# Routed attention and a squared-ReLU MLP on one core: v products in even units of batch 0's second half, plain products in odd ones

## The chip, the cores and the metric

The kernel runs on one core of a Trainium2 chip. The metric is the time of one execution on the device in microseconds (us), the median of five runs. Before the change it is 978.76 us (976.63 to 979.76).

## The reference, cut to what matters

```python
q, k, v: (4, 8, 768, 64)   centroids: (8, 16, 64)   w_in: (512, 2048)   w_out: (2048, 512)
q_assign = argmax(q_n . c_n)          # each query and key belongs to one of 16 clusters
k_assign = argmax(k_n . c_n)
scores = where(q_assign == k_assign, q @ k.T / sqrt(64), -1e9)
attn = exp(scores - max);  attn = attn / (sum(attn) + 1e-9)
x = (attn @ v), heads side by side    # (3072, 512)
out = relu(x @ w_in) ** 2 @ w_out     # (3072, 512)
```

## The kernel before

**Units.** A pair is two heads of one batch: 16 pairs, pairs 0 to 3 are batch 0 (`HP` = 4). The 768 queries of a pair are cut in two halves `h`, the keys in three steps `c` of 256. A unit is (pair, h, c). The list `units` (L718) has the first halves of pairs 0 to 3 (units 0 to 11), then their second halves (12 to 23; `TWOS` = 12), then pairs 4 to 15 with both halves (24 to 95). The main loop at L786 goes through the units. For each it writes, in this order, the score products and exponentials, the v products that are ready, the sums that are complete, the rounding of weights, and some "plain" products.

**Scores** (`scores`, L446). TensorE makes eight products into two PSUM tiles `sc`. ScalarE takes the exponential (L473). In batch 0 the mask is inside the products (one-hot `ohT`), and the exponential writes the tile `ex`, of which there are three buffers. From pair 4 on, the mask is four VectorE operations (L477) which write `ex` and read `qid`, a tile that the preparation of the pair sends through DRAM (`spread`, L400). GpSimd adds up `ex` into `acc` (L487, L489).

**v products** (`times_v`, L504). Four products for each unit, into `av`, accumulated over the three units of a half. The PSUM pool has two such tiles.

**Sums** (`add_up`, L530, and `finish`, L560). When a half is complete, TensorE multiplies the sums by ones into a PSUM bank `sm`, VectorE takes the reciprocal `r` (L544), the SP queue sends it to DRAM (`far_r`, L547, and `seen`, L551) and back spread over the partitions (`rb`, L550), and VectorE multiplies (L563) and so writes `xT`. This L563 also frees the `av` tile.

**Plain products** (`ffn`, L572). The two halves of batch 0 go through the MLP by ordinary matrix products: 64 of 384 columns into a bank `ph` for each half (L577, each followed by two ScalarE operations for every four), then 48 of 512 columns into `po` (L590). They need only `xT` and weights, and `fill_steps` deals them out in columns. `density` says how many parts of them a unit gets: 4 in batch 0, 2 later. The other batches run after the loop (`ffn_pair`, L603).

**Banks.** `sm`, `ph`, `po`, `lg`, `lt` and `pb` share one pool of two PSUM banks (`ps_f`, L79). A product into a new bank waits until the bank before last has been read.

**Rounding of weights** (`round_weights`, L141). 32 blocks, 4 in every 3 units from the start up to unit 23. Each takes two ScalarE operations (L150, L152), three VectorE operations (L155, L159, L162), one GpSimd addition (L166), and then frees one of four buffers `w_raw`, into which the SP queue loads the next block (L139).

**Preparation of a pair** (`prep`, L415). For pair 4 it is a list of fifteen items, three taken in each unit: the transposed load of q and k (`turn_words`, L290), the splitting of the next pair's words (L273), the cluster products `lg` (`logits`, L300), the choice of the cluster (`route`, L313: transposes into `lt`, then VectorE's L344 to L363), and `spread` (transpose `pb`, ScalarE L407, `far` L409, `qid` L410).

**What sets the order.** Each engine, and the SP queue, works in a fixed order which a scheduler makes from the program's order, dependencies and priorities (`together` gives products a high one). An instruction that waits holds up all that stands behind it on its engine or queue. Two places of the loop set which units do what:

```python
elif u == TWOS or u % 2 or u >= len(units):      # L804: v products up to unit u - 1
    ready = u
if u % 2 == 0 or not TWOS < u < len(units):      # L841: plain products for two units
```

So after unit 12 an odd unit has the v products of two units and no plain products, and an even unit has plain products for two units and no v products.

Of the kernel before, what the change touches and what calls it, by code (L numbers as in the profile page):

```python
# [25 lines left out]
def kernel(  # L26
# [14 lines left out]
    NCH = S // P  # L41
# [4 lines left out]
    HP = H // 2  # L46
# [68 lines left out]
    def load_v(pair):  # L115
        b, hp = divmod(pair, HP)
        raw_v[pair] = loads_v.tile([P, 2, NCH, D], F32, name="v_raw")
        nc.sync.dma_start(
            raw_v[pair], v[b, 2 * hp : 2 * hp + 2].rearrange("h (p j) d -> p h j d", p=P)
        )  # L120
# [16 lines left out]
    def load_weights(i):  # L137
        raw_w[i] = wstage.tile([P, NW, 2], U32, name="w_raw")
        nc.sync.dma_start(raw_w[i], weights[i][1])  # L139
# [133 lines left out]
    def split_words(pair, which):  # L273
        if which == 0:
            words[pair] = dram.tile([2 * NCH, P, 2, 2 * D], U16, name="words")
        flat = loads.tile([P, NCH, 2, 2 * D], U16, name="flat", tag="qk")
        src = raw[pair][which].bitcast(U16).rearrange("p c (d two) -> p c two d", two=2)
        half = NCH // 2
        with tc.issue_after(last_exp[0]):
            for cols in (slice(0, half), slice(half, NCH)):  # L280
                nc.scalar.copy(out=flat[:, cols], in_=src[:, cols])
        nc.sync.dma_start(
            words[pair][NCH * which : NCH * (which + 1)].rearrange("c p two d -> p c two d"),
            flat,
        )
        if which == 1:
            raw.pop(pair)
            load_qk(pair + 1)
# [126 lines left out]
    def prep(pair):  # L415
        if pair < HP:
            return [
                lambda: turn(pair, 0), lambda: turn(pair, 1), lambda: turn(pair, 2),
                lambda: logits(pair), lambda: route(pair),
                lambda: turn_onehot(pair, 0), lambda: turn_onehot(pair, 1),  # L420
            ]

        split = [lambda i=i: split_words(pair + 1, i) for i in range(2 if pair + 1 < NG else 0)]
        first, second = split or (None, None)
        return [
            lambda: turn_words(pair), None, None, first, None, None,
            lambda: logits(pair), None, lambda: route(pair), second, None, None,
            None, None, lambda: spread(pair),
        ]
# [10 lines left out]
    def first_half(pair, h):  # L440
        return pair < HP and h == 0
# [62 lines left out]
    def times_v(pair, h, c):  # L504
        if c == 0:
            av[pair, h] = ps_av.tile([P, TB], F32, name="av", tag="av")
            if first_half(pair, h):
                sums[pair, h] = ps_av.tile([P, TB // 2], F32, name="sm", tag="av")
        t = ex.pop((pair, h, c))
        products = [  # L510
            dict(
                out=av[pair, h][D * e : D * (e + 1)], lhsT=raw_v[pair][:, e, c + i],
                rhs=t[:, 2 * i + e], start=(c + i == 0), stop=(c + i == NCH - 1),
            )
            for i in range(2) for e in range(2)
        ]
        if first_half(pair, h):
            for i in range(2):
                one = [
                    ones_products(  # L520
                        sums[pair, h], e, t[:, 2 * i + e], c + i == 0, c + i == NCH - 1
                    )
                    for e in range(2)
                ]
                products += [p for both in zip(*one) for p in both]
        together(products, 4000)
# [76 lines left out]
    def ffn_pair(pools, b):  # L603
# [114 lines left out]
    units = [  # L718
        (pair, h, c)
        for pairs, halves in [(range(HP), [0]), (range(HP), [1])]  # L720
        + [([pair], [0, 1]) for pair in range(HP, NG)]
        for pair in pairs for h in halves for c in range(0, NCH, 2)
    ]
# [6 lines left out]
    TWOS = HP * NCH // 2  # L730

    ENDS = len(units) + 2

    def density(u):


        return 4 if u < HP * NCH else 2 if u < len(units) - NCH else 3

    def fill_steps(columns):

        while fill and columns > 0:
            if (passed := next(fill[0], None)) is None:
                fill.pop(0)
            else:
                columns -= passed
                left[0] -= passed

    def behind_first(u, what=last_logits):
        return tc.issue_after(what[0]) if u == 0 else ExitStack()

    def next_pair(u):

        pair, h, c = units[u]
        if c == 0 and pair + 1 < NG and h == 0 and (pair + 1) not in qkT:
            if pair + 1 < HP or pair >= HP:
                return pair + 1
        if u == TWOS + 4:
            return HP
        return None

# [16 lines left out]
    def ends(halves):  # L777
        for pair, h in halves:
            b, hp = divmod(pair, HP)

            with tc.high_priority(offset=1000) if (pair, h) == (HP - 1, 0) else ExitStack():
                finish(pair, h)
            if hp == HP - 1 and (b, h) in PLAIN:
                fill.append(ffn(b, h))

    for u in range(len(units) + 3):  # L786
        if u < len(units):
            pair, h, c = units[u]
            if (p := next_pair(u)) is not None:
                ahead.extend(prep(p))  # L790
            if u in (TWOS, TWOS + 2):

                split_words(HP, int(u > TWOS))
            if c == 0 and u + 3 < len(units) and units[u + 3][0] not in raw_v:
                load_v(units[u + 3][0])

            with behind_first(u):
                scores(pair, h, c)

        ends(added)  # L800
        added.clear()
        if u < TWOS:
            ready = u - 1
        elif u == TWOS or u % 2 or u >= len(units):  # L804
            ready = u

        complete, late = late, []
        while v_next < min(ready, len(units)):
            pair, h, c = units[v_next]
            times_v(pair, h, c)  # L810
            v_next += 1
            if c == NCH - 2:
                (late if h and not HP * NCH <= u < len(units) else complete).append((pair, h))
        for pair, h in complete:
            with tc.high_priority(offset=1000) if first_half(pair, h) else ExitStack():
                add_up(pair, h)
            if h == 1:
                for d in (qkT, ids, qid):
                    d.pop(pair)
            if h == 1 or pair < HP:  # L820
                raw_v.pop(pair)
            added.append((pair, h))

        rounding += 4
        while rounding >= 3:
            rounding -= 3
            i = next(to_round, None)
            if i is not None:
                with tc.issue_after(last_exp[0]):
                    round_weights(i)  # L830
                if (i := next(loaded, None)) is not None:
                    load_weights(i)
            elif not later:
                early.close()
                for name, bufs in (("xT", 5), ("out", 2)):
                    later[name] = keep.enter_context(
                        tc.tile_pool(name=name + "_late", bufs=bufs, side="right",
                                     reuse_waits="tile")
                    )
        share = 0  # L840
        if u % 2 == 0 or not TWOS < u < len(units):  # L841
            n = 2 if TWOS < u < len(units) else 1
            share = max(0, left[0] - RESERVE) * sum(map(density, range(u, u + n)))
            share //= max(1, sum(map(density, range(u, ENDS))))
        goal = left[0] - share

        for i in range(3):
            if i == 2:
                fill_steps(share * 2 // 3)
            if ahead:  # L850
                with behind_first(u, masked if i else last_logits):
                    (ahead.pop(0) or int)()
        fill_steps(left[0] - goal)
# [235 lines left out]
```

## Time and profile before

| | us |
|---|---|
| median of five runs | 978.76 |
| the profiled execution's own time | 981.31 |
| its span, first to last instruction | 979.5 |
| TensorE busy in the span | 958.7 |
| VectorE, ScalarE, GpSimd busy | 563.8, 315.7, 378.0 |
| TensorE waiting for an engine, longest: for `xT` (L563) | 4.2 |

The second half of batch 0 is the stretch from about 75 us (unit 12) to 160 us (unit 24). Times in the text are us from the span's start. "96.15 to 97.97" means that the next group of products starts at 97.97: this distance is the price of the first group, since a product's own duration overlaps the next one.

### The profile page before, as it was taken

The numbers are of one execution on the slowest core, as the hardware profiler recorded it, in microseconds if no ns is written. First come the engines' busy times: TensorE is split into PE (matmuls) and PEld (weight loads), VectorE is DVE, ScalarE is ACT, GpSimd is POOL, SyncE is SP. The second block draws the span as 40 slices with busy tenths as digits, with TensorE's granted clock in tenths as the row PEclk, the third lists the DMA queues.
The fourth block names the chain that finished last, engine by engine and source line by source line (L and its number), as shares of the span: only waits on it lengthen the run. The fifth ranks groups of instructions, "written<-read, shape, count | busy, mean of one in ns | idle before, by whom it ended". The sixth has DMA issues, their size and how long they took to land.

```text
span 979.5 us, 12067 instructions
## 1 busy us (share of the span) xinstructions
PE 958.7 (98%) x4479; PEld 551.8 (56%) x4479; DVE 563.8 (58%) x913; ACT 315.7 (32%) x511; POOL 378.0 (39%) x277
## 2 busy tenths in 40 slices
PE   8998999999999999999999999999999999999997
PEld 4543444443444444444443555888556888556886
DVE  5768767665656656666657966531556531656331
ACT  5885756444435555544331111000111000111000
POOL 1337756555555666565567431002231002231000
PEclk9998999999999999999999999999999999999999
DMA  9757681544545455453310000000000000000000
GB/s 247 210 179 202 183 203 43 126 117 116 133 113 129 120 117 120 110 130 82 83 38 16 20 1 0 12 22 26 7 1 1 22 22 21 1 1 0 22 22 25
DMA packets 127746, 74.54 MB, mean 76 GB/s; under 512 B 90944, under 2 KB 119104, under 8 KB 127680
## 3 DMA queue, kind: packets, MB, share of 16 engines
q1 hardware_dynamic: 125968, 73.26, 28.5%
q8 instruction: 38, 0.62, 0.3%
q10 hardware_dynamic: 1712, 0.43, 0.2%
q14 instruction: 28, 0.23, 0.1%
HBM read 48.27 MB, written 15.86 MB: 65 GB/s over the span
## 4 chain that ended last, share of the span: by engine, by line
PE 88%; DMA 4%; DVE 2%; issue 2%; POOL 1%; SPq 1%; ACT 1%; ACTq 0%; DVEq 0%; POOLq 0%
PE bank L700 22%; PE bank L669 22%; PE ph L577 8%; PE po L590 8%; PE sc L91 7%; PE sc L94 6%; PE av L91 6%; PE av L94 5%; PE sm L91 1%; DMA rb<-far_r 1%; PE lg L91 1%; POOL w_in L166 1%; DMA qid<-far 1%; SPq L292 1%; DVE ex L477 1%
## 5 line engine op out<-in xcount | busy, mean ns | idle before, releaser
L489 POOL TENSOR_TENSOR acc<-acc,ex 128x768 f32<-128x768 f32 x112 | 205.7, 1836 | 106.6 <-DVE ex L477 93.5
L477 DVE SCALAR_TENSOR_TENSOR ex<-qid,ids,sc 128x384 f32<-128x384 bf16 x288 | 157.8, 608 | 64.3 <-ACT sc L473 40.5
L473 ACT ACTIVATE sc<-sc 128x768 f32<-128x768 f32 x144 | 108.5, 792 | 160.2 <-PE sc L94 139.9
L94 PE MATMUL sc<-qkT 64*128 64x384 f32 x576 | 152.4, 503 | 0.6
L94 PE MATMUL av<-ex,v_raw 128*64 128x384 f32 x576 | 135.5, 491 | 0.0
L658 POOL TENSOR_TENSOR w_s<-w_in 128x256 f32<-128x256 f32 x24 | 18.2, 756 | 273.9 <-PE bank L700 162.0
L639 DVE TENSOR_TENSOR g<-bank,g 128x384 f32<-128x384 f32 x144 | 77.8, 555 | 79.1 <-PE bank L669 77.9
L577 PE MATMUL ph<-xT,w_in 128*128 128x384 f32 x256 | 94.5, 511 | 4.9 <-DVE xT L563 4.2
L700 PE MATMUL bank<-w_out,g 128*128 128x256 f32 x432 | 95.2, 379 | 0.0
L590 PE MATMUL po<-w_out,gT 128*128 128x512 f32 x192 | 91.7, 609 | 0.0
L91 PE MATMUL sc<-qkT 64*128 64x384 f32 x192 | 87.2, 534 | 2.7 <-DVE ex L477 2.6
L700 PEld LDWEIGHTS bank<-w_out,g 128*128 128x128 f32 x432 | 82.1, 190 | 11.8
L639 DVE TENSOR_TENSOR osb<-bank,osb 128x256 f32<-128x256 f32 x54 | 22.1, 423 | 107.6 <-PE bank L700 102.2
L94 PEld LDWEIGHTS sc<-qkT 64*128 64x128 f32 x576 | 65.0, 186 | 27.8 <-issue 6.0
L91 PE MATMUL av<-ex,v_raw 128*64 128x384 f32 x192 | 80.4, 500 | 0.0
L577 PEld LDWEIGHTS ph<-xT,w_in 128*128 128x128 f32 x256 | 47.1, 195 | 45.3 <-issue 14.3
L487 POOL TENSOR_TENSOR acc<-ex 128x768 f32<-128x768 f32 x28 | 50.9, 1816 | 52.9 <-DVE ex L477 38.3
L669 PE MATMUL bank<-xT,w_in 128*128 128x384 f32 x192 | 69.9, 487 | 0.0
L669 PE MATMUL bank<-x_t,w_s 128*128 128x384 f32 x192 | 69.8, 486 | 0.0
L669 PE MATMUL bank<-xT,w_s 128*128 128x384 f32 x192 | 69.8, 486 | 0.0
L94 PEld LDWEIGHTS av<-ex,v_raw 128*64 128x64 f32 x576 | 49.5, 137 | 34.2 <-issue 34.0
L700 PE MATMUL bank<-w_t,g 128*128 128x256 f32 x288 | 65.1, 379 | 0.0
(127 smaller groups left out, 1221.9 us busy)
## 6 DMA issues: line engine op xcount, KB each, us to landing
words<-flat SPq DMA_DIRECT2D x24, 384.0 KB
w_raw<-in_moe_w_in_dram SPq DMA_DIRECT2D x16, 512.0 KB
w_raw<-in_moe_w_out_dram SPq DMA_DIRECT2D x16, 512.0 KB
v_raw<-in_v_dram SPq DMA_DIRECT2D x20, 384.0 KB
rb<-far_r SPq DMA_DIRECT2D x64, 96.0 KB
q_raw<-in_q_dram SPq DMA_DIRECT2D x31, 192.0 KB
k_raw<-in_k_dram SPq DMA_DIRECT2D x31, 192.0 KB
out_dram<-osb SPq DMA_DIRECT2D x23, 256.0 KB
```

Source lines behind the costliest of these rows:

```text
L91: last = nc.tensor.matmul(**next(products))
L94: last = nc.tensor.matmul(**product)
L473: last_exp[0] = nc.scalar.activation(out=t[:, 2 * i : 2 * i + 2] if pair < HP else src, in_=src, func=ACT.Exp, scale=SCALE).ins
L477: last_mask[0] = nc.vector.scalar_tensor_tensor(out=t[:, 2 * i + e], in0=qid[pair][1][:, h, e], scalar=ids[pair][:, ch % NB, 2 + ch // NB, ...
L487: nc.gpsimd.tensor_tensor(out=acc[pair, h], in0=t[:, 0:2], in1=t[:, 2:4], op=ALU.add)
L489: nc.gpsimd.tensor_tensor(out=acc[pair, h], in0=acc[pair, h], in1=t[:, 2 * i : 2 * i + 2], op=ALU.add)
L577: nc.tensor.matmul(ph, lhsT=w_in[:, kk, f * P : (f + 1) * P], rhs=xT[b, h][:, kk], start=(kk == 0), stop=(kk == KT - 1),)
L590: nc.tensor.matmul(po, lhsT=gT[f][:, i * P : (i + 1) * P], rhs=w_out[:, f], start=(f == 0), stop=(f == FT - 1),)
L639: nc.vector.tensor_tensor(out=out, in0=bank, in1=to, op=ALU.add)
L658: nc.gpsimd.tensor_tensor(out=s1, in0=a[1][0], in1=a[1][1], op=ALU.add)
L669: nc.tensor.matmul(bank, lhsT=operands[j][0][:, kk], rhs=operands[j][1][:, kk], start=(kk == 0), stop=(kk == H2 - 1),)
L700: nc.tensor.matmul(bank, lhsT=operands[j][0][:, f], rhs=operands[j][1][:, f], start=(f == 0), stop=(f == F2 - 1),)
```

## The change

```diff
+    def values_in(u):
+        if u < HP * NCH:
+            return u < TWOS + 2 or u % 2 == 0
+        return u % 2 == 1
...
-        if u == TWOS + 4:
+        if u == TWOS + 5:
             return HP
...
-        elif u == TWOS or u % 2 or u >= len(units):
+        elif u == TWOS or values_in(u) or u >= len(units):
             ready = u
...
-        if u % 2 == 0 or not TWOS < u < len(units):
+        if not values_in(u) or not TWOS < u < len(units):
             n = 2 if TWOS < u < len(units) else 1
```

In units 14 to 23 the v products now stand in the even units and the plain products in the odd ones; from unit 25 on all is as before. The preparation of pair 4 begins in unit 17 instead of 16. Units 13 and 14 have the v products of one unit each. Units 23 and 24 have none, so that unit 25 has those of units 22, 23 and 24.

The order of TensorE's instructions in the two built programs, by units (S the score products of a unit; V and the number of the unit whose v products follow; sm, lg, lt, pb as above; PH and a count for products into `ph`):

| unit | before | after |
|---|---|---|
| 12, 13 | S V10 V11; S V12 | the same |
| 14 | S PH11 | S V13 |
| 15 | S V13 V14 | S PH11 |
| 16 | S sm PH1 | S V14 V15 |
| 17 | S PH10 V15 V16 | S sm PH1 |
| 18 | S lg PH2 | S PH10 V16 V17 |
| 19 | S PH6 lt PH2 V17 PH1 V18 | S sm PH2 |
| 20 | S sm PH7 pb | S lg PH6 lt PH2 V18 PH1 V19 |
| 21 | S PH4 V19 V20 | S PH7 pb |
| 22 | S sm PH11 | S PH4 V20 V21 |
| 23 | S V21 V22 | S sm PH8 |
| 24 | S PH6 | S PH6 |
| 25 | S V23 V24 sm | S V22 V23 V24 sm |

The fourth product of the PH11 is the first that needs the last part of `xT`, from the `finish` of pair 3's first half. The count of every kind of product is the same in both programs; later some plain products stand one unit earlier or later, and before the last sum of the loop three products into `po` stand in place of two. On VectorE the order around the change becomes:

| | before | after |
|---|---|---|
| first sum (pair 0) | blocks A, reciprocal | blocks A, B, reciprocal |
| second sum (pair 1) | choice of the cluster, reciprocal, two blocks, L563 | reciprocal, two blocks, L563, one block, choice of the cluster |
| third sum (pair 2) | L563, two blocks, masks of unit 24 | two blocks, L563, masks of unit 24 |

Block A is the one rounded in unit 15, block B that of unit 16. On the SP queue, in both programs, a load L139 that waits for GpSimd's addition stands ahead of `far_r` of pair 0, and one ahead of each of the `rb` of pairs 0 and 1. The transposed load for pair 5, which before stands several DMAs ahead of `far` and `qid` of pair 4, stands directly ahead of them after the change.

## Prediction

> **What bounds the kernel now.** I read the shares of the engines first, then the waits of TensorE, then its timeline with the granted clock at the longest wait, then VectorE's timeline there.
>
> ```profile
> PE 958.7 (98%) x4479; PEld 551.8 (56%) x4479; DVE 563.8 (58%) x913; ACT 315.7 (32%) x511; POOL 378.0 (39%) x277
> ...
> PEclk9998999999999999999999999999999999999999
> ```
>
> ```profile
> PE ph L577 <- DVE xT L563: 4.2, 1, 4.2
> ...
> PE sc L91 <- DVE ex L477: 2.6, 3, 1.4
> ...
> PE sm L91 <- POOL acc L489: 1.6, 1, 1.6
> ...
> PE ph L577 <- DVE best L345: 0.7, 1, 0.7
> ```
>
> TensorE (PE) is busy for 98%. The change leaves its products as they are, so only its idle time (some 20 us in all) and its clock can move. Slice 4 (73 to 98 us) is the only one whose granted clock falls to 0.8; the longest wait lies in it.
>
> ```profile
> 87.87 8.35 PE L577 MATMUL ph<-xT,w_in 128*128 128x384 f32 x16 [4.16 <-DVE xT L563]
> ...
> 96.15 0.59 PE L91 MATMUL sc<-qkT 64*128 64x384 f32 x1
> ...
> 97.97 0.54 PE L91 MATMUL av<-ex,v_raw 128*64 128x384 f32 x1
> ...
> 100.70 0.59 PE L91 MATMUL sc<-qkT 64*128 64x384 f32 x1
> ...
> 105.63 6.72 PE L577 MATMUL ph<-xT,w_in 128*128 128x384 f32 x20
> ```
>
> ```profile
> 86.00:88.00 2.00, 0.13 (x1) 0.16 (x1) 1.90 (x2) 0.00 (x0) 1.31 (x1) 0.75 0.84 281
> ...
> 88.00:90.00 2.00, 2.00 (x4) 1.08 (x5) 1.93 (x5) 0.47 (x1) 0.80 (x1) 0.50 0.69 152
> ...
> 93.00:94.00 1.00, 1.00 (x3) 0.56 (x2) 1.00 (x2) 0.00 (x0) 1.00 (x1) 0.59 0.97 328
> ```
>
> The fourth product of unit 14 waits from 83.71 to 87.87 for xT. After that the clock (third figure from the right in the last three lines) is 0.50. Its 0.75 over 86 to 88 puts the fall at 87.0, its 0.59 over 93 to 94 the return at 93.8. The distances give prices: a unit's scores (S) 97.97 - 96.15 = 1.82, two units' v products 100.70 - 97.97 = 2.73, ten ph products from 105.63 to 112.28, so 0.665 each. Eight such products after the wait took 8.28 (to 96.15) in place of 5.32: 2.96 lost to the clock.
>
> ```profile
> 86.10 1.63 DVE L563 SCALAR_TENSOR_TENSOR xT<-xT,rb 128x384 f32<-128x384 f32 x1 [3.83 <-ACT w_raw L152]
> ...
> 89.50 1.39 DVE L159 TENSOR_SCALAR w_out<-w_out 128x512 uint32<-128x512 uint32 x1
> ...
> 90.81 2.29 DVE L162 SCALAR_TENSOR_TENSOR w_raw<-w_raw 128x512 uint32<-128x512 uint32 x1
> ...
> 100.08 1.58 DVE L155 TENSOR_SCALAR w_out<-w_out 128x512 f32<-128x512 f32 x1 [3.00 <-ACT w_out L150]
> ...
> 103.11 1.36 DVE L544 RECIPROCAL r<-sm 128x192 f32<-128x192 f32 x1 [0.38 <-PE sm L94]
> ...
> 127.56 0.56 DVE L344 TENSOR_REDUCE mx<-lt 128x24 f32<-128x384 f32 x1
> ```
>
> VectorE (DVE) does rounding blocks of three operations whenever it can. The same L159 takes 0.43 at 88.09, and 1.39 here, where GpSimd adds beside it (89.20 to 90.60). What matters after the change is how many such operations stand ahead of what TensorE waits for.
>
> **The gain: the wait for xT is filled.** S14 ends at 81.51. After the change V13 (half of 2.73, 1.37) follows, to 82.9. S15 reuses the score tiles that the exponentials of unit 14 read; the first of these runs on ScalarE until 83.1, so S15 runs from 83.1 to 84.9. The first three ph products (2.0) end at 86.9, xT comes at 87.73 as before, for its chain goes through the DMA rb and no edit touches that. Idle left: 0.2 + 0.8 = 1.0, against 4.16: **-3.1**. With no long idle the clock stays up: **-2.96** in a run that has the halving.
>
> **First cost: unit 18 waits for the reciprocal of pair 0.** PH10 takes the bank that holds the sums sm, free once L544 has read them. TensorE now comes there at 87.87 + 5.32 (PH8) + 1.82 (S16) + 2.73 (V14, V15) + 1.82 (S17) + 0.46 (sm) + 0.67 (PH1) + 1.82 (S18) = 102.5. VectorE finishes the earlier blocks at 97.08 as before, but now has blocks A and B ahead of the reciprocal. In the profile those six operations take 2.65 (100.08 to 102.73) and 4.22 (104.62 to 108.84), together 6.87; started at 97.08, the reciprocal ends at 97.08 + 6.87 + 1.36 = 105.3, a wait of 2.8. Lower bound: six at the mean of the nine in 87.65 to 97.08 (1.05 each) gives 104.7, so 2.2. Upper: the six from 108.76 to 116.42 take 7.66, 3.6; if block B's input from ScalarE, which stands behind the exponentials of unit 16, is 0.6 late besides, 4.2. I take the middle of 2.8 and 4.2: **+3.5**. Nothing covers it: the products behind stand in fixed order.
>
> The Trainium skill speaks against the change here: "SBUF — State Buffer", section "Terms", has VectorE and GpSimd share a port pair by an exclusive lock held for a whole instruction, the loser blocking fully. The rows 1.39 and 2.29 beside GpSimd agree in kind. By the rule any operation here that needs the pair can be held for one GpSimd addition (1.84 each in the page), so that the sum would use the upper end, 4.2, and be 0.7 higher; by the rows, where most operations beside GpSimd are not held, it stays at 3.5.
>
> **Second cost: unit 20 waits for the choice of the cluster.** A product into ph after V18 takes the bank of lt, which L344 and L345 read. Now L563 of pair 1 stands ahead of these, and its rb comes by DMA. TensorE leaves the first wait at 106.0; PH10 6.65, V16 V17 2.73, S19 1.82 bring sm to 117.2 to 117.7, PH2 1.33, S20 1.82, lg 0.78, PH6 4.0, lt 0.33, PH2 1.33 and V18 1.37 the bank's next use to 128.6. VectorE's reciprocal of pair 1 ends near 119.5 (1.36 and a small rest). On SP's queue rb stands behind an L139 that waits for GpSimd's addition of unit 19's block: its exponential ends near 118.6, ScalarE's two operations 119.8, VectorE's three 124.5 (behind the reciprocal and another block), GpSimd's addition, 1.3 and perhaps behind a 1.84 one, 126.4. From rb's issue to the start of L563 the trace has 3.3 (152.24 to 155.58), 5.0 (81.07 to 86.10) and 5.3 (141.17 to 146.44). Then L563 0.56, a block alone 1.4, L344 and L345 1.15: 3.1. So 126.4 + 3.3 + 3.1 = 132.8 at the nearest landing, 134.8 at the farthest: waits of 4.2 and 6.2. If that addition doesn't hold the queue and rb goes at 124.5, 2.3. The addition is the weakest link, so I take a value near the shortest landing: 4.6, and less the 0.74 of the present wait **+3.9**.
>
> **Smaller parts.** The wait of 1.43 at 166.75 goes: now sm and PH8 stand between S23 and unit 24 in place of V21 V22 (5.8 against 2.7), more than the 1.43 and the L563 of 0.56 that VectorE gets in addition; cover left 1.1: **-1.4**. Before the loop's last sum, three po products instead of two give GpSimd 0.92 more: **-0.9** of 1.6. The preparation one unit later sends qid's DMA behind pair 5's transposed load on SP (4.1 of SP's time): pb near 141, then SP 4.1, far and qid 2.3 to 4.4 and 3.6 to 4.2 as the other pairs' rows have them, 151 to 154, before unit 24's masks near 157: nothing, with some 3 to 6 of cover; beyond it masks and scores of unit 25 are late one for one. Two units' masks (VectorE, 0.55 each) wait for ex buffers that V22 frees in unit 25; V23 and V24 (2.7) cover them: nothing, up to 1 if not. Clock: the 4.16 wait dropped it 3.3 after its beginning (83.71 to 87.0). The second wait, 4.6, counts like it: **+2.96** against the -2.96. The first, 3.5, barely reaches: between 0 and 2.96, a tenth taken, **+0.3**.
>
> **Sum:** -3.1 - 2.96 + 3.5 + 3.9 - 1.4 - 0.9 + 2.96 + 0.3 = **+2.3**. The profiled execution took 981.31 (span 979.5), 2.55 above the median 978.76; that is about one halving, so the runs may differ by just this. As the halving is on both sides of the sum, I put it on the median: 978.76 + 2.3, about **981.0** (+0.23%).
>
> "TensorE: Matmul & The Clock Gate", section "Part 1: The HAM clock gate (the "warmup" mystery)", gives a free-running window of about 3.4 us that must be idle for the clock to halve. The 0.50 after a wait of 4.16 agrees. By it, as an estimate, a wait of 4.16 holds a whole window in some 2 runs of 10 and one of 4.6 in 3 or 4; the exchange would cost 0.4 in place of 0.3, hardly another sum.
>
> **The rivals.** A measurement of this kernel can tell about 0.2% (2 us) from no change.
> (1) *Faster.* Both new waits are at their lower ends: -3.1 + 2.2 + (2.3 - 0.7) - 1.4 - 0.9 = -1.6, with neither halving the clock and the 2.96 won in the runs that had it: 974.2 to 977.2. For: the six operations alone take 1.5 a block. Against: GpSimd is busy in nearly all of 100 to 116. Chance 0.28.
> (2) *Much slower*: rb of pair 1 held on SP's queue. If it is issued 2 later than 124.5 and lands in 5.3, that wait is 6.2 (+5.5), the first is 4.2, both halve: -3.1 - 2.96 + 4.2 + 5.5 - 1.4 - 0.9 + 5.9 = +7.2, 984 to 986. It decides once both waits exceed about 4. For: two landings of three are 5 or more. Against: the first wait needs its upper end as well. Chance 0.13.
> (3) *Idle time only changes place*: S15 waits longer for the tiles, or xT comes later since other DMA is ahead, so the gain is about 2, and the waits that follow shrink as much, being aligned to VectorE, not to TensorE: 977 to 980.5. Chance 0.17.
>
> **Numbers.** Forecast 0.42, own range 979 to 983: slower 0.28, same 0.14. Rival 1: faster 0.24, same 0.04. Rival 2: slower 0.13. Rival 3: same 0.10, faster 0.02, slower 0.05. Sums: faster 0.26, same 0.28, slower 0.46. The range reaches into rivals 1 and 2 until about 1 in 10 is left out at each end: 975.5 to 984.5.
>
> **What would show it.** In TensorE's waits: L577 on L563 gone or near 1; a new one on the reciprocal L544 near 103 of 2.2 to 4.2; the one on L345 near 129 grown to 2.3 to 6.2; the one on L477 near 167 gone; sm on L489 down to 0.7. Granted clock 1.0 in 87 to 94 and, if I am right, 0.5 for some us after 130. I am wrong if VectorE reaches the reciprocal of pair 0 before 102, if rb of pair 1 leaves before 123, or if unit 24's masks wait for qid.

## The result and the profile after

The changed kernel takes 982.51 us (median of 37 runs, 979.17 to 987.80), the kernel before beside it 978.64 (63 runs, 975.71 to 984.71): a ratio of 1.0040, 95% interval 1.0031 to 1.0049, or 3.9 us more. The profiled execution of the changed kernel took 981.67 with a span of 979.9, only 0.4 more than the span of the profile before. So the two profiles alone do not show the loss; why is the first thing to explain.

The waits of TensorE in the changed kernel (us in total, times, longest):

```profile
PE ph L577 <- DVE best L345: 4.0, 1, 4.0
PE ph L577 <- DVE r L544: 3.6, 1, 3.6
...
PE sm L91 <- POOL acc L489: 0.7, 1, 0.7
...
PE sc L91 <- DVE ex L477: 0.6, 2, 0.3
```

The wait for xT is gone, the one on L477 near 167 too. Two waits of almost 4 us are new, both for VectorE, in the places that the prediction named. TensorE's timeline has them at 101.4 to 105.05 and at 129.7 to 133.65:

```profile
84.56 7.39 PE L577 MATMUL ph<-xT,w_in 128*128 128x384 f32 x22
...
105.05 8.41 PE L577 MATMUL ph<-xT,w_in 128*128 128x384 f32 x20 [3.62 <-DVE r L544]
...
133.65 1.62 PE L577 MATMUL ph<-xT,w_in 128*128 128x384 f32 x2 [3.97 <-DVE best L345]
```

The ten products after the first wait last 8.41, where the same ten took 6.72 before. The stretches say why (the granted clock is the third figure from the right):

```profile
102.00:104.00 2.00, 0.00 (x0) 0.00 (x0) 2.00 (x2) 1.97 (x5) 1.92 (x2) 1.00 1.39 295
104.00:106.00 2.00, 0.95 (x2) 0.65 (x3) 1.97 (x3) 1.38 (x2) 2.00 (x2) 0.81 0.75 241
106.00:108.00 2.00, 2.00 (x4) 1.02 (x4) 2.00 (x2) 1.12 (x2) 2.00 (x2) 0.50 0.80 224
108.00:110.00 2.00, 2.00 (x6) 1.09 (x5) 2.00 (x2) 1.20 (x3) 1.92 (x2) 0.83 0.63 242
...
132.00:134.00 2.00, 0.35 (x1) 0.38 (x2) 1.93 (x5) 0.00 (x0) 1.28 (x1) 0.64 0.76 238
134.00:136.00 2.00, 2.00 (x6) 0.52 (x7) 0.95 (x3) 0.00 (x0) 0.00 (x0) 0.50 0.54 125
136.00:138.00 2.00, 2.00 (x10) 0.41 (x6) 0.00 (x0) 0.00 (x0) 0.00 (x0) 0.50 0.99 326
138.00:140.00 2.00, 2.00 (x10) 1.09 (x10) 0.00 (x0) 0.00 (x0) 0.00 (x0) 0.65 1.23 279
```

With both waits comes half clock: 3.4 us of it from 105.2 on, as the first wait ends, and 6.8 from 132.6 on, the last 1.1 us of the second wait included. VectorE (the third busy figure: 2.00, 1.97, 2.00, 2.00 from 102 to 110) is almost never idle around the first. Its timeline shows what it did instead of the reciprocal and of L344:

```profile
84.16 2.16 DVE L563 SCALAR_TENSOR_TENSOR xT<-xT,rb 128x384 f32<-128x384 f32 x1 [3.30 <-DMA rb<-far_r]
...
100.09 1.41 DVE L159 TENSOR_SCALAR w_out<-w_out 128x512 uint32<-128x512 uint32 x1
101.42 2.31 DVE L162 SCALAR_TENSOR_TENSOR w_raw<-w_raw 128x512 uint32<-128x512 uint32 x1
103.65 1.34 DVE L544 RECIPROCAL r<-sm 128x192 f32<-128x192 f32 x1
...
130.46 0.56 DVE L563 SCALAR_TENSOR_TENSOR xT<-av,rb 128x384 f32<-128x384 f32 x1 [2.16 <-DMA rb<-far_r]
...
132.94 0.56 DVE L345 TENSOR_TENSOR best<-lt,mx 128x384 bf16<-128x384 f32 x1
```

Block B ends at 103.7, and only then comes the reciprocal; L563 of pair 1 waits for its rb until 130.46, and L345 stands behind it and one block. L563 of pair 3, which writes xT, began 1.9 us earlier than in the profile before (84.16 against 86.10), which no edit explains. That leads to the first experiment.

### The profile page after: what moved, and what is told of

Same layout as the page of the kernel before. It is cut to its first block, busy times and chain, and to the rows that moved or that the text cites. A ratio compares the mean times of both kernels' runs of the same rounds, so it can differ in the third digit from the quotient of the medians.

```text
span 979.9 us, 12066 instructions
## 1 busy us (share of the span) xinstructions
PE 960.3 (98%) x4479; PEld 552.4 (56%) x4479; DVE 566.8 (58%) x913; ACT 315.7 (32%) x511; POOL 379.2 (39%) x277
## 4 chain that ended last, share of the span: by engine, by line
PE 87%; DVE 4%; DMA 3%; ACT 3%; issue 1%; POOL 1%; SPq 0%; ACTq 0%; DVEq 0%; POOLq 0%
PE bank L700 22%; PE bank L669 22%; PE ph L577 8%; PE po L590 7%; PE sc L91 7%; PE sc L94 6%; PE av L91 6%; PE av L94 5%; DMA rb<-far_r 2%; ACT ex L473 1%; PE sm L91 1%; DVE w_raw L162 1%; PE sm L94 1%; POOL acc L489 1%; DVE ex L477 1%
## 5 line engine op out<-in xcount | busy, mean ns | idle before, releaser
L489 POOL TENSOR_TENSOR acc<-acc,ex 128x768 f32<-128x768 f32 x112 | 206.3, 1842 | 107.7 <-DVE ex L477 98.9
L477 DVE SCALAR_TENSOR_TENSOR ex<-qid,ids,sc 128x384 f32<-128x384 bf16 x288 | 157.9, 609 | 68.3 <-ACT sc L473 42.6
```

What stands on the lines that cost most here:

```text
L477: last_mask[0] = nc.vector.scalar_tensor_tensor(out=t[:, 2 * i + e], in0=qid[pair][1][:, h, e], scalar=ids[pair][:, ch % NB, 2 + ch // NB, ...
L489: nc.gpsimd.tensor_tensor(out=acc[pair, h], in0=acc[pair, h], in1=t[:, 2 * i : 2 * i + 2], op=ALU.add)
```

## The experiments

Every kernel below was timed beside the kernel before; ratios are to that, with their 95% interval. "Mean clock" is the mean over its runs of the TensorE clock granted over the span, recorded in each run.

**The kernel before, once more.** No edit.

> The kernel before, unchanged, to see how its runs differ. Theory A (its wait of 4.16 us for xT halves the clock in about every run): mean granted clock about 0.996 in nearly all runs, as in the first profile, where 6.8 us at half clock are 0.0035 of the span. Theory B (only in some runs): many runs at 0.998 or more, and these about 3 us shorter. Time the same as before within 0.1%.

Ratio 0.9996 (0.9984 to 1.0007). Of 46 runs of this kernel in that comparison, 27 had a clock of 0.998 or more, 19 less; these 27 took 978.3 on the mean, the 19 took 980.0. In the two later comparisons it was 12 of 29 and 17 of 35. The second profile (976.87 us, span 975.0) has these waits:

```profile
PE sc L91 <- DVE ex L477: 2.7, 4, 1.4
PE ph L577 <- DVE best L345: 1.8, 1, 1.8
PE sm L91 <- POOL acc L489: 1.6, 1, 1.6
...
PE ph L577 <- DVE r L544: 1.3, 1, 1.3
...
PE ph L577 <- DVE xT L563: 0.9, 1, 0.9
```

The wait for xT is 0.9, not 4.2, no stretch from 80 to 168 us is at half clock, and the reciprocal and L345 are each waited for already. VectorE's L563 stands at 83.55 here. So the size of the largest wait in the profile before belonged to that execution, whose 981.31 lies above all five runs shown and whose clock of 0.996 is that of few: 14 of these 110 runs have 0.996 or less. (This second one, at 976.87, is on the other side of the median; in the run with the later preparation alone, below, whose order is the same up to there, the wait for xT is 1.8.) Theory B holds, but the difference is 1.8 us, not 3.

Between this execution and the profiled one of the changed kernel the spans differ by 4.9. The waits give: reciprocal 3.62 - 1.33 = +2.3, L345 3.97 - 1.75 = +2.2, xT -0.9, L477 0.6 - 2.7 = -2.1, sm 0.7 - 1.6 = -0.9, together +0.6. The rest is the clock: PH10 with V16 and V17 take 11.07 (105.05 to 116.12) in place of 6.65 + 2.73, so 1.7 lost; PH1 and V19 after the second wait take 4.31 in place of 2.26 (124.70 to 126.96 here), the scores of unit 21 2.50 in place of 1.82, so 2.7 lost; +4.4. Sum +5.0.

**Block B in unit 17**, so that the reciprocal of pair 0 stands ahead of it.

```diff
-        rounding += 4
+        rounding += {TWOS + 4: 1, TWOS + 5: 7}.get(u, 4)
```

> The changed kernel, with block B rounded in unit 17, so that VectorE takes the reciprocal of pair 0 ahead of it. Theory A (each new wait stands by itself): the wait of 3.6 us on the reciprocal falls to 0 to 0.6, the half clock after it goes (1.7 us), the wait on L345 stays near 4: about 5 us shorter than the changed kernel, 0.999 of before. Rival R (VectorE's and GpSimd's rounding is the bound in this stretch): the first wait goes, but the wait on L345 grows by the same 3 to 4 us, since VectorE's work ahead of it is the same, and the ratio to before stays at 1.002 to 1.005.

Ratio 1.0035 (1.0022 to 1.0047), as slow as the changed kernel. Its waits:

```profile
PE ph L577 <- DVE best L345: 5.8, 1, 5.8
PE ph L577 <- ACT gT L584: 1.6, 1, 1.6
...
PE lg L91 <- DVE r L544: 1.1, 1, 1.1
```

The wait of unit 18 is gone, and the one on L345 has grown from 4.0 to 5.8, with new ones of 1.6 and 1.1 between. Rival R's outcome came: TensorE, earlier at the first gate (a point where it must wait for another engine), waits longer at the next, which opens when it did before (L345 ends at 133.28, in the changed kernel at 133.50). Its reason holds only in part. VectorE is idle ahead of L563 of pair 1:

```profile
130.39 0.56 DVE L563 SCALAR_TENSOR_TENSOR xT<-av,rb 128x384 f32<-128x384 f32 x1 [2.57 <-DMA rb<-far_r]
```

So here rb holds L345. It was issued at 125.76, behind a load L139 that waits for GpSimd's part of the rounding (L166, 123.89 to 125.30).

**L563 of pair 1 behind L345.** One instruction moved on VectorE (`number` keeps the instruction of L345 in `last_number[0]`):

```diff
-            with tc.high_priority(offset=1000) if (pair, h) == (HP - 1, 0) else ExitStack():
+            with tc.high_priority(offset=1000) if (pair, h) == (HP - 1, 0) else tc.issue_after(last_number[0]) if (pair, h) == (1, 1) else ExitStack():
```

> The changed kernel, with VectorE's L563 of pair 1 moved behind L345, nothing else. If that L563 (waiting for rb) is what holds the choice of the cluster: the wait on L345 falls from 4.0 to about 1.2 (L344 can start when the block before it ends, near 129.7), the half clock after it goes (3.4 us), the wait on the reciprocal stays at 3.6: ratio to before 0.998 to 1.001. If the rounding block is what holds it: the wait stays above 3, ratio 1.003 to 1.005.

Ratio 1.0034 (1.0022 to 1.0046): no gain. VectorE's timeline:

```profile
125.01 2.30 DVE L162 SCALAR_TENSOR_TENSOR w_raw<-w_raw 128x512 uint32<-128x512 uint32 x1
127.23 2.03 DVE L155 TENSOR_SCALAR w_out<-w_out 128x512 f32<-128x512 f32 x1
129.19 1.76 DVE L162 SCALAR_TENSOR_TENSOR w_raw<-w_raw 128x512 uint32<-128x512 uint32 x1
130.88 0.42 DVE L159 TENSOR_SCALAR w_out<-w_out 128x512 uint32<-128x512 uint32 x1
131.21 0.55 DVE L344 TENSOR_REDUCE mx<-lt 128x24 f32<-128x384 f32 x1
```

The block that I had put at 1.4 begins at once, but beside GpSimd's additions (124.76 to 130.4) it takes 4.0. L344 comes at 131.21 in place of 132.36, so L345 is done 1.15 earlier; but TensorE is 1.7 earlier too (at 127.98), as no half clock followed its first wait, and with rb alone taken away the wait is 4.5. rb and the rounding hold L345 nearly equally long.

**Both edits.**

> Both edits, block B later and L563 of pair 1 behind L345. Theory A: neither wait is left over 1.5 us, no half clock between 80 and 160 us, about 7 to 10 us shorter than the changed kernel: ratio to before 0.993 to 0.997. Rival R: the wait on L345 still 3 or more, ratio 0.999 to 1.002.

Ratio 1.0025 (1.0011 to 1.0040), with waits of 3.7 on L345 and 1.8 on the reciprocal of pair 1. VectorE's lag stays.

**V13 alone moved into the wait**, the kernel before otherwise.

```diff
-        elif u == TWOS or u % 2 or u >= len(units):
+        elif u in (TWOS, TWOS + 2) or u % 2 or u >= len(units):
```

> The kernel before, with V13 moved from unit 15 to unit 14, ahead of the products that wait for xT, and nothing else: the order on every other engine stays. Theory C (the wait for xT is 0.9 to 4.2 us by execution and is what halves the clock in about 4 of 10 runs of before, mean clock 0.998): the wait is 0 to 2.8, the mean clock rises to 0.999 or more, the time falls by 1 to 2.5 us, ratio 0.9975 to 0.999. Rival (the clock of before is lost elsewhere, or another wait takes the 1.4 us): mean clock stays near 0.998, ratio 0.9995 to 1.001.

Ratio 0.9998 (0.9984 to 1.0012): theory C's gain did not come. In its profile:

```profile
PE sc L91 <- DVE ex L477: 3.0, 3, 1.5
PE ph L577 <- DVE r L544: 2.6, 1, 2.6
PE ph L577 <- DVE best L345: 1.8, 1, 1.8
...
PE ph L577 <- DVE xT L563: 0.9, 1, 0.9
```

The wait on the reciprocal is 2.6, against 1.3 in the second profile of the kernel before; the one for xT is 0.9 in both, since xT came later in this execution. From the end of the wait for xT to the end of the one on the reciprocal it is 16.2 us in both (85.88 to 102.04, 84.26 to 100.47): VectorE sets that distance, and of the 1.4 us of V13, which TensorE no longer has in between, it waits off 1.2. The mean clock, 0.9979, is within the scatter of the kernel before (0.9972 beside it, 0.9979 and 0.9977 in the other two comparisons).

**Without GpSimd's additions L489 in batch 0.** The second and third unit of each half are left out of its sums.

```diff
-        for i in range(2 if c else 0):
+        for i in range(2 if c and pair >= HP else 0):
```

> The changed kernel without GpSimd's additions L489 in batch 0 (the second and third unit of a half are left out of the sums). If VectorE's lag comes from its rounding running beside GpSimd's additions (1.4 to 2.3 us an operation in place of 0.4 to 0.7): both new waits below 1 us, no half clock between 80 and 160 us, mean clock 0.999, about 9 us shorter than the changed kernel, ratio 0.993 to 0.996. If the count of rounding blocks in the order of VectorE sets it: waits of 2 us or more stay, ratio 1.000 to 1.003.

Ratio 0.9907 (0.9889 to 0.9925), mean clock 0.9987: 11 us less than the changed kernel by the medians, 13 by the ratios, more than expected. VectorE is through with block B before the reciprocal is wanted:

```profile
96.94 0.41 DVE L155 TENSOR_SCALAR w_out<-w_out 128x512 f32<-128x512 f32 x1
97.39 1.39 DVE L159 TENSOR_SCALAR w_out<-w_out 128x512 uint32<-128x512 uint32 x1
98.70 0.68 DVE L162 SCALAR_TENSOR_TENSOR w_raw<-w_raw 128x512 uint32<-128x512 uint32 x1
99.33 1.36 DVE L544 RECIPROCAL r<-sm 128x192 f32<-128x192 f32 x1
```

The same block took 4.0 beside the additions and 2.4 here; the wait on the reciprocal is nothing, the one on L345 1.2. By the two profiles the time is won between 85 and 140 us: unit 15's plain products start 0.4 later than in the changed kernel, unit 21's 10.2 earlier. So this stretch is bound by VectorE's rounding and GpSimd's additions together. The run does not part two ways in which the additions cost: they hold up single operations of VectorE, and they delay GpSimd's part of the rounding and with it rb (issued at 118.64 here, at 126.25 in the changed kernel). The first shows in the rows: in the first profile of the kernel before, from 76 to 130 us, the 11 rounding operations of VectorE that overlap no GpSimd addition take 0.36 to 0.69 each, and 16 of the 20 that overlap one take 1.4 to 2.3.

**The two parts of the change apart.** First the parity alone (`u == TWOS + 4`), in two comparisons, then the later preparation alone in the kernel before.

> The changed kernel with the preparation of pair 4 beginning in unit 16 again, so the parity alone. If the long wait on L345 comes from the later preparation: L345 stands ahead of the second reciprocal again, that wait falls to below 2, the wait on the reciprocal of pair 0 stays near 3.6; one halving instead of two, mean clock about 0.996, ratio 1.001 to 1.003. If the parity alone brings VectorE's lag: another wait of 3 us or more on VectorE between 115 and 140 us, ratio 1.003 to 1.006.

> The parity alone (preparation in unit 16), once more for its interval: 0.9975 to 1.0007 before, I expect 0.998 to 1.000, mean clock 0.996.

> The kernel before with the preparation of pair 4 a unit later, nothing else. If the later preparation alone moves the choice of the cluster against VectorE's queue: a changed wait on L345, the one of the reciprocal of pair 0 as in before (1 to 2). No theory of mine has it cheaper by more than 1 us or dearer by more than 3: ratio 0.999 to 1.003.

The parity alone: 0.9991 (0.9975 to 1.0007) and 0.9997 (0.9983 to 1.0012), not to be told from no change; I had expected 1.001 to 1.003. TensorE waits 3.7 and 3.1 for the reciprocal of pair 0 and nowhere long for L345, which now comes ahead of the second reciprocal; mean clock 0.996. The later preparation alone: 1.0019 (1.0006 to 1.0033). Its profile has no wait on L345; its largest is one of 2.1 for unit 24's masks (L477), until 165.22. Added, the parts give about 1.001; together they gave 1.0040. The loss needs both: only with the parity does the later choice of the cluster fall behind the second sum on VectorE.

**The blocks moved to where VectorE was idle.** The changed kernel idles on VectorE from 135.0 to 142.6 and from 145.2 to 149.2. Block B goes to unit 21, and in the second and third version a block of unit 17 to unit 22:

```diff
-        rounding += 4
+        rounding += {TWOS + 4: 1, TWOS + 5: 1, TWOS + 9: 7, TWOS + 10: 7}.get(u, 4)
```

> The parity with the preparation in unit 16, and block B rounded in unit 21, where VectorE was idle for 6 us. If block B ahead of the reciprocal is the whole of the wait of 3.7 us: that wait falls to 0 to 0.7 and takes its half clock along, nothing long follows (the choice of the cluster stands ahead of the second sum), mean clock 0.998 to 0.999, ratio 0.993 to 0.996. If VectorE's lag only moves on, as with block B in unit 17: another wait of 2 us or more on VectorE before 160 us, ratio 0.997 to 1.000.

> As the one before, with one block of unit 17 moved to unit 22 as well. If VectorE is the bound up to 118 us: not slower than with one block moved, within 1 us of it, ratio 0.993 to 0.996. If the later blocks run into the masks of unit 24: a wait on L477 of 1 to 4 us near 165, ratio 0.996 to 1.000.

> The changed kernel (preparation in unit 17) with block B moved to unit 21 and a block of unit 17 to unit 22. If the rounding blocks ahead of the reciprocal and of L345 make both new waits: the first 0 to 0.7, the second below 2, mean clock 0.998 or more, ratio 0.994 to 0.997. If the later preparation costs for another reason (rb of pair 1, or the queue): the wait on L345 stays above 3, ratio 0.999 to 1.002.

With the parity alone: one block 0.9973 (0.9960 to 0.9987), two blocks 0.9966 (0.9952 to 0.9979, 975.36 us), both faster than the kernel before and the changed one, and not to be told apart. With one block the wait on the reciprocal fell to 0.4, as the first theory had it, but the time fell less than it said; the profile, of 972.46, is that of the fastest of its 12 runs. The blocks were not moved in the kernel before, so how much of this gain needs the parity is open. With two blocks only this wait is left between 76 and 175 us, by TensorE's timeline:

```profile
150.07 2.85 PE L577 MATMUL ph<-xT,w_in 128*128 128x384 f32 x8 [2.13 <-DVE r L544]
```

With the whole change (the third version) 0.9984 (0.9971 to 0.9997): the first wait is gone, the second stays at 4.0, now with VectorE idle ahead of it.

```profile
127.99 0.56 DVE L563 SCALAR_TENSOR_TENSOR xT<-av,rb 128x384 f32<-128x384 f32 x1 [2.67 <-DMA rb<-far_r]
...
130.32 0.56 DVE L345 TENSOR_TENSOR best<-lt,mx 128x384 bf16<-128x384 f32 x1
```

So with the preparation in unit 17 there are two chains of nearly the same length ahead of L345, the rounding and rb of pair 1. Removing either alone leaves the other; removing both at once in the changed kernel was not tried.

## Why the prediction was right or wrong

**Sign and size.** +2.3 us was forecast, 981.0; measured were +3.9 and 982.51, in the forecast's own range of 979 to 983. Several terms were off and partly made up for each other; that the time lies in the range is in part luck.

**The gain from the wait for xT** was the term most mis-sized: -3.1 and -2.96 are what the profiled execution had to give; the second profile has 0.9 and no half clock there, the run with the later preparation alone 1.8 and none. I saw that this execution lay 2.55 above the median and named the halving as its likely cause, but kept the term for the median, since "the halving is on both sides of the sum". It was not, or not equally: in every recorded run of the changed kernel the clock is 0.996 or less; of the 110 of the kernel before in the three comparisons, 96 are above that.

**The first cost** came out near, 3.62 against 3.5, with errors that cancelled: the six operations took 8.0 (95.65 to 103.65) in place of 6.87, but began 1.4 earlier, as xT had come earlier, with TensorE 1.1 earlier too (101.4). Two readings of rows were wrong there. The stretch from 108.76 to 116.42 holds five operations, not six; with the sixth, behind L563, it is 8.07. And it is not so that most operations beside GpSimd are not held: 16 of 20 were. The upper end of 4.2, which the prediction did not take because of these rows, has the six at 8.3, nearer to the 8.0. Against the second profile of before, which waits 1.3 there, the cost is +2.3. The half clock after it, for which I took a tenth (0.3), cost 1.7 here; of the four profiles in which this wait is 3.1 to 3.7, three have it.

**The second cost**: the wait of 3.97 against 4.6, and link by link the chain holds: rb issued at 126.25 (forecast 126.4), L563 4.2 later (3.3 taken), then 3.0 to the end of L345 (3.1); TensorE came at 129.7, not 128.6. Against 1.75 in the second profile of before it is +2.2 in place of +3.9. What I missed is that VectorE's blocks, by themselves, end nearly as late (L344 at 131.21 with L563 behind it, in place of 132.36).

**The smaller parts** held: the wait near 167 is gone, sm waits 0.7, and unit 24's masks follow directly on VectorE's other work (163.54), so qid was not late. The waits on L477 as a group fell by 2.1, more than 1.4.

**The clock.** Taking (1 - mean clock) x span for the time lost, an estimate that is right where TensorE is the bound, the changed kernel loses 5.6 us, the kernel before 2.0 to 2.7 in its comparisons. By this estimate 2.9 to 3.6 of the 3.9 are clock: the idle time as such hardly changed (+0.6 between the two profiles above), but most of it stands in two pieces, and both came with half clock in the profile.

**The rivals.** Rival 3's mechanism, waits aligned to VectorE so that time won ahead of it is waited off behind it, is what the block in unit 17 and V13 alone showed; its times, 977 to 980.5, did not come, since the order also put more of VectorE's work ahead of TensorE's gates.

## What to carry to other kernels

Before a wait in one profile is priced, look whether that execution is a usual one: here its time above the median and the clock recorded in each run told that its largest wait was not. Filling a wait of the busiest engine paid nothing here, since the engine that it waits for next was full: look at that engine's timeline behind the gap, and move its work into its own idle time first. And idle time is not all alike: nearly the same sum, most of it in two pieces of 4 us, cost some 3 us more (the estimate from the clock) than in pieces of 1 to 2.

## What the runs showed of the hardware

The half clock lasts 3.4 us or twice that at every wait that I measured, but what starts it is not simply the length of a wait. The wait on the reciprocal of pair 0 was followed by it at 3.62 (the changed kernel), 3.68 and 3.11 (the parity alone), and not at 3.54 (L563 behind L345). In the run with V13 alone, a wait of only 1.76 us (124.52 to 126.28) was followed by it:

```profile
124.00:126.00 2.00, 0.52 (x4) 0.00 (x0) 1.97 (x3) 0.16 (x1) 1.37 (x2) 1.00 0.74 154
126.00:128.00 2.00, 1.72 (x8) 0.77 (x10) 1.55 (x4) 0.00 (x0) 0.44 (x1) 0.92 0.25 33
128.00:130.00 2.00, 2.00 (x8) 0.62 (x6) 0.00 (x0) 0.00 (x0) 0.00 (x0) 0.50 0.88 259
```

So were one of 1.76 with both edits (ending at 120.70) and one of 2.06 with the later preparation alone (ending at 165.22), the clock falling each time within 1.5 us of the wait's end. In the second profile of the kernel before, a wait of 1.75 at the same place (ending at 124.70) was not, nor was the 2.57 of V13 alone. The Trainium skill ("TensorE: Matmul & The Clock Gate", section "Part 1: The HAM clock gate (the "warmup" mystery)") has a free-running window of about 3.4 us that must be idle; the durations agree with such a window, the waits of 1.76 and 2.06 do not agree with a wholly idle one. And the landing of the same small transfer differs between executions of one program: from the issue of rb of pair 3 to the start of L563 it took 5.0 in the first profile of the kernel before (81.07 to 86.10), 4.2 in the second (79.31 to 83.55) and 3.7 with V13 alone (81.14 to 84.86).
